# Gated mix of two attention branches: features stored with their sign innermost, key weights transposed while loading, and a new order of steps

## The chip, the core and the metric

The kernel runs on one core of a Trainium2 chip. Its engines work side by side, each through its own queue in order: PE (matmul; a weight load stands before each matmul and may run beside the one ahead), DVE (vector), ACT (activation), POOL (GpSimd), and SP, which issues most of the DMAs. The metric is the device time of one execution in microseconds (us), as a median over runs. The span of a profile is the time from the first instruction of the program to the last.

## What is computed

One input x of 2048 rows by 640 is sent through two attention branches of 32 heads of 20 columns each; a gate for each row mixes the results.

```python
x = A_x
g = _sigmoid((x * gate_w).sum(-1, keepdims=True))
a = _A_ref(x, A_wqkv, A_w_phi, A_wo)        # linear branch
b = _B_ref(x, B_wq, B_wk, B_wv, B_wo, B_beta)   # memory branch
return g * a + (1 - g) * b

# linear branch, for each head
pk = einsum('bhsd,hdf->bhsf', k, w_phi)          # pq likewise
phi_k = concatenate([softmax(pk), softmax(-pk)])  # over the 20 features
kv = einsum('bhsf,bhsd->bhfd', phi_k, v)
z = einsum('bhsf->bhf', phi_k)
o = (phi_q @ kv) / (phi_q @ z + 1e-6)

# memory branch, for each of 4 segments of 512 rows
p = softmax(q @ k.T * scale + causal mask within the segment)
o = sig(beta) * (phi(q) @ M) / (phi(q) @ z) + (1 - sig(beta)) * (p @ v)
M, z = M + phi(k).T @ v, z + sum(phi(k))
```

## The kernel before

The rows of x are cut into 16 chunks of 128; the memory branch works in four segments of four chunks. x is held transposed (`xT`: five blocks of 128 columns by 2048 rows), loaded by transposing DMAs.

All work after the first loads is written as steps. The list `ORDER` (L773) is a hand-fixed sequence of words: the first letter names a function (table `STEPS`, L762), the digit its step, and what follows a PSUM slot or `a` for an eviction on ACT instead of DVE. The n-th occurrence of a word works on the n-th item. Instructions are kept in program order (`Kept`, L98), so the list sets the order on every engine's queue. All instructions are issued through that helper, so the profile shows L104 for nearly all of them, and groups are told apart by the names of their tiles.

Steps of the linear branch (A), by their words:

- T (`transposed`): the key weights `WkN`, loaded plainly, are transposed on PE in 25 blocks and evicted into `WkT`. F and W (`fold`): the key and query weights are multiplied with `w_phi` (`Wphi`, in windows of up to eight heads for each 128 rows), giving `WkA` and `WqA`. The query weights come transposed by DMA (D, `load_q`).
- A (`key`, L244): for each chunk, step 0 projects x with `WkA` (ten matmuls of 320 columns into `k_ps`), steps 1 and 2 take the exponential with scale 1 and -1 on ACT into `Ek`, step 3 sums over a head's 20 features on DVE, step 4 takes the reciprocal, step 5 multiplies into `phk`. B (`value`) projects the values into `vA`, with the row gate as column 321.
- S (`sums`): z, by 160 matmuls of 4 columns with blocks of `phk` as weights (`zb_ps`). s (`blocks`): adds them up on DVE. X (`products`): kv, for each of five blocks of 128 features and each sign 16 matmuls with `phk` as weights (`kv_ps`), masked to the own head's columns by `hm`.
- f (`features`): the query features, kept transposed in `ET`; d (`weights`): denominators; n (`numerators`): for each chunk and half of the heads three matmuls for each sign (`num_ps`).

Steps of the memory branch (B): k, K, v, q project keys, values and queries (`proj`, `q_ps`); P (`scores`) computes causal score blocks `st_ps`, their exponentials on ACT (`PT`, 128 x 1024) and the mask on POOL; V (`attended`) sums with the values (`nd_ps`); Y and M hold the memory term. l, o write the output; t, b, p, a, e, h are the last rows. G, O and J compute gates; I masks.

In `phk` and `Ek` the two signs lie in separate halves. Within a half, the heads are stored in pairs, feature by feature, the two heads of a pair innermost (`"p s (b f i)"`, f = 20, i = 2). The evictions of the folds bring the weights' columns into that order, and the mask `hm` is made from pair masks (`blk`) and a parity (`par`), the latter from the identity matrix that also serves the transposes. A block of 128 stored columns touches eight heads, so the windows of X and n (`WIN`, L163) are eight heads or 160 columns wide (80 where the heads' halves part).

The first loads go out in this order on SP's queue: xT for 128 rows, xT for 384 rows, then L118 to L125: `WkN`, `Wc` (w_phi), `stq` (Wq of the memory branch, which POOL copies in another column order into `WqB`, L159), `WvB`, `WvA`, gate, beta. `WkB` goes out on ACT's queue. L (`load_x`) loads the other three quarters of xT.

Of the kernel before, what the change touches and what calls it, by code (L numbers as in the profile page):

```python
# [8 lines left out]
ALU = mybir.AluOpType  # L9
# [6 lines left out]
def kernel(  # L16
# [64 lines left out]
    phk = apool.tile([P, NCH, 2, D], BF16, name="phk")  # L81
# [3 lines left out]
    late = phk.rearrange("p c s n -> p (c s n)")[:, 16 * D:32 * D]  # L85
    WkN = late[:, 0:KC * D].rearrange("p (c n) -> p c n", c=KC)
# [31 lines left out]
    for out_, in_ in ((WkN, rows5(A_wqkv[:, D:2 * D])),  # L118
                      (Wc, rows5(A_w_phi.rearrange("h f g -> (h f) g"))),
                      (stq, rows5(B_wq)),  # L120
                      (WvB, rows5(B_wv)),
                      (WvA[:, :, 0:D], rows5(A_wqkv[:, 2 * D:3 * D])),
                      (WvA[:, :, D:D + 1], gate_w.rearrange("(c p o) -> p c o", p=P, o=1)),
                      (beta_b, B_beta.partition_broadcast(P))):
        syn.dma_start(out=out_, in_=in_)  # L125

    NW = 8
# [4 lines left out]
    for n in range(WARM):  # L132
        ten.matmul(wu, lhsT=wz[:, 0:P], rhs=wz, start=True, stop=True)
    gps.memset(kpads[:, :, :, DH:32], 0.0)
    ident_f = apool.tile([P, P], F32, name="ident_f")
    gps.memset(ident_f, 0.0)
    gps.affine_select(out=ident_f, in_=ident_f, pattern=[[-1, P]], compare_op=ALU.not_equal,
                      fill=1.0, base=0, channel_multiplier=1)
    gps.memset(kp2[:, :, :, DH:32], 0.0)
    ident = apool.tile([P, P], BF16, name="ident")  # L140
    vec.memset(qTp[0], 0.0)
    vec.tensor_copy(out=ident, in_=ident_f)
# [14 lines left out]
    blk = apool.tile([P, KC, NW // 2], F32, name="blk")  # L157
    band(blk, 8, 2 * DH, NW // 2)
    for c in range(KC):  # L159
        gps.tensor_copy(out=WqB[:, c, :].rearrange("p (r g) -> p r g", g=G),  # L160
                        in_=stq[:, c, :].rearrange("p (g r) -> p r g", g=G))

    WIN = []  # L163
    for c in range(KC):
        lo, hi = 6 * c, 6 * c + NW
        if lo < 16 < hi:
            WIN += [(c, lo, 16), (c, 16, hi)]
        else:
            WIN.append((c, lo, hi))
    FIRST = {w: all((w[1] // 16) != (v[1] // 16) for v in WIN[:n]) for n, w in enumerate(WIN)}  # L170
    LAST = {w: all((w[1] // 16) != (v[1] // 16) for v in WIN[n + 1:]) for n, w in enumerate(WIN)}
# [36 lines left out]
    for k, eps in enumerate((9.98377799987793e-07, 1.622538547962904e-09, -3.410605131648481e-13)):  # L208
        den = Msb.rearrange("p g i e -> p (g i) e")[:, :, DH].rearrange("p (g i) -> p g i", i=4)
        gps.affine_select(out=den, in_=den, pattern=[[0, G], [-32, 4]], compare_op=ALU.not_equal,  # L210
                          fill=eps, base=-(DH + k), channel_multiplier=1)

    gl = const.tile([P, NCH], F32, name="gl")
    par = const.tile([P, 2], F32, name="par")
# [29 lines left out]
    def key(n, step, at, ev):  # L244
# [5 lines left out]
        elif step < 3:  # L250
            if step == 1:
                t.E = a1w.tile([P, 2, D], BF16, name="Ek")
            sca.activation(out=t.E[:, step - 1, :].rearrange("p (a n) -> p a n", a=2),
                           in_=t.ps[:, :, 0:320], func=ACT.Exp, scale=1.0 if step == 1 else -1.0)
        elif step == 3:
            t.Ev = t.E.rearrange("p s (b f i) -> p (s b) f i", f=DH, i=2)
            t.sum = a1w.tile([P, H, 2], F32, name="ksum")
            vec.tensor_reduce(out=t.sum, in_=t.Ev.rearrange("p b f i -> p b i f"),
# [5 lines left out]
        else:  # L264
            vec.tensor_tensor(
                out=phk[:, n].rearrange("p s (b f i) -> p (s b) f i", f=DH, i=2),
# [12 lines left out]

    def transposed(n, step, at, ev):  # L280
        t = item("T", n)
        if step == 0:
            t.ps = bank([P, KC, P], "tp_ps", at, BF16)
            for c in range(KC):
                ten.transpose(out=t.ps[:, c, :], in_=WkN[:, n, c * P:(c + 1) * P], identity=ident)
        else:
            ev(out=WkT[:, :, n * P:(n + 1) * P], in_=t.ps)

    def fold(kind, dst, WT):
        def run(n, step, at, ev):  # L290
# [9 lines left out]
            else:  # L300
                b = step - 1
                ev(out=dst[:, n, b * 320:(b + 1) * 320].rearrange("p (b f i) -> p b i f", f=DH, i=2),
                   in_=t.ps[:, b, 0:320].rearrange("p (b i f) -> p b i f", f=DH, i=2))
        return run

    def masks(n, step, at, ev):
        if step == 0:
            vec.tensor_tensor(
                out=Wphi, in0=Wc[:, :, None, :].to_broadcast([P, KC, NW, DH]),
                in1=hn_f[:, :, :, None].to_broadcast([P, KC, NW, DH]), op=ALU.mult)  # L310
            return
        vec.tensor_reduce(
            out=par, in_=ident_f.rearrange("p (a i) -> p i a", i=2), axis=AX.X, op=ALU.add)
        vec.tensor_tensor(
            out=hm.rearrange("p c (b i) -> p (c b) i", i=2),
            in0=blk.rearrange("p c b -> p (c b)")[:, :, None].to_broadcast([P, KC * NW // 2, 2]),
            in1=par[:, None, :].to_broadcast([P, KC * NW // 2, 2]), op=ALU.mult)
        vec.tensor_copy(out=ind, in_=bd01)
        for sg in range(2):
            vec.tensor_copy(out=HZ[:, :, sg, 0, :], in_=hm)  # L320

    def beta_gate(n, step, at, ev):
        if step == 0:
            sca.activation(out=sig_b, in_=beta_b, func=ACT.Exp, scale=-1.0)
            return
        vec.tensor_scalar(out=sig_b, in0=sig_b, scalar1=1.0, scalar2=None, op0=ALU.add)
        vec.reciprocal(out=sig_b, in_=sig_b)
        vec.tensor_scalar(out=omgh_b, in0=sig_b, scalar1=-1.0, scalar2=1.0,
                          op0=ALU.mult, op1=ALU.add)
        vec.tensor_copy(out=CM[:, :, :, DH:DH + 1],  # L330
                        in_=bd01[:, None, :, None].to_broadcast([P, G, 4, 1]))
        vec.tensor_tensor(
            out=CM[:, :, :, 0:DH],
            in0=sig_b.rearrange("p (g i) -> p g i", i=4)[:, :, :, None].to_broadcast([P, G, 4, DH]),
            in1=bd01[:, None, :, None].to_broadcast([P, G, 4, DH]), op=ALU.mult)

    def token_gate(s, step, at, ev):
        n = slice(4 * s, 4 * s + 4)
        if step == 0:
            sca.activation(out=rgS[:, n], in_=gl[:, n], func=ACT.Exp, scale=-1.0)  # L340
            return
        vec.tensor_scalar(out=rgS[:, n], in0=rgS[:, n], scalar1=1.0, scalar2=None, op0=ALU.add)
        vec.reciprocal(out=omgS[:, n], in_=rgS[:, n])
        vec.tensor_scalar(out=omgS[:, n], in0=omgS[:, n], scalar1=-1.0, scalar2=1.0,
                          op0=ALU.mult, op1=ALU.add)
# [6 lines left out]
    def sums(n, step, at, ev):  # L352
        sgn, half = divmod(n, 2)
        t = item("S", sgn)
        if step == 0:
            if half == 0:
                t.ps = bank([P, KC, 4 * NCH], "zb_ps", at)
            for sc in range(half * NCH // 2, (half + 1) * NCH // 2):
                for c in range(KC):
                    ten.matmul(t.ps[:, c, 4 * sc:4 * sc + 4], lhsT=phk[:, sc, sgn, c * P:(c + 1) * P],  # L360
# [18 lines left out]
    def products(n, step, at, ev):  # L379
        t = item("X", n)  # L380
        c, sgn = divmod(n, 2)
        if step == 0:
            t.ps = bank([P, NW, DH], "kv_ps", at)
            for sc in range(NCH):
                ten.matmul(t.ps, lhsT=phk[:, sc, sgn, c * P:(c + 1) * P],
                           rhs=vA[:, sc, 6 * c * DH:(6 * c + NW) * DH],
                           start=(sc == 0), stop=(sc == NCH - 1))
        else:
            vec.tensor_tensor(out=KV[:, c, sgn], in0=t.ps,
                              in1=hm[:, c, :, None].to_broadcast([P, NW, DH]), op=ALU.mult)  # L390
# [141 lines left out]
    def numerators(n, step, at, ev):  # L532
        s, j, b = n // 8, n % 8 // 2, n % 2
        t = item("n", n)
        if step < 2:
            nm = bank([P, 320], "num_ps", at)
            for w in WIN:
                c, lo, hi = w
                if lo // 16 == b:
                    ten.matmul(nm[:, (lo - 16 * b) * DH:(hi - 16 * b) * DH],  # L540
                               lhsT=item("E", s).t[:, step, c, j * P:(j + 1) * P],
                               rhs=KV[:, c, step, lo - 6 * c:hi - 6 * c, :],
                               start=FIRST[w], stop=LAST[w], skip_group_check=True)
# [208 lines left out]
    def tail_out(j, step, at, ev):  # L752
# [9 lines left out]
    STEPS = dict(A=key, B=value, T=transposed, F=fold("F", WkA, WkT), W=fold("W", WqA, WqT), I=masks,  # L762
# [11 lines left out]
        "k00 k01 k1 k02 k1 K0 K1 k03 k1 k00 K2 k1 k01 k1 k1 T02 I0 T03 k00 T1a T1 T01 k1 F00 F01 "  # L774
        "T1 F1a T02 L0 F1 T03 F2a F2 T1a F00 T1 k00 F1a F2a F01 k1 F00 F1 v01 F1a F2 F2a v02 v1 "
        "k2 K0 K1 A01 v1a K2 L0 v03 A1 A00 v1 A2 A3 A01 A1 A2 D0 A4 q00 A1 A3 A2 k01 q1a A5 A00 "
        "A3 K0 A01 A1 A4 k1 q02 A2 K1 A4 A5 k03 q1a K2 A00 A3 A1 A2 k2 B00 A5 B11 k1 A1 q2 A01 A3 "
        "B2a k2 B3a A2 B02 A4 q2 B4 A4 B13 A3 B2a v00 K0 k2 B01 B3a A5 v1a B12 B2a K1 A00 B4 A5 "
        "A1 B3a A4 A2 K2 v00 A1 B4 A5 W01 q03 A2 A3 v1a W1a B01 W2a A3 B12 q1a B2a A00 q2 B3a A4 "
        "B4 A4 G0 q00 A5 A1 G1 A2 A01 A5 q1a q2 A3 B03 A1 B11 A2 B2 B02 A4 B3a B4 B10 A3 B2a L0 "  # L780
        "W00 W01 B3a B03 B4 W1 W1a W2a W2 B11 A4 B2a W01 B3 A00 B4 W1 W2 A01 A1 A2 q02 A3 W00 v00 "
        "q1a I1 W1a B03 q2 W2a B11 v1a A4 B2a B02 A5 B3a B10 B4 A5 A1 A00 G0 B2 A2 A5 B3a v03 B4 "
        "A1 G1 q01 A3 A2 v1a P01 B02 A3 q1a P1 B10 B03 A4 P2 P3 B2 B11 A4 K0 P4 B3 P01 B2a v02 B4 "
        "A5 B3a P1 B00 K1 B4 A5 B13 P2 P3 v1 A01 B2 B3a P4 B4 G0 G1 J0 A00 A1 J1 A2 B01 A1 B12 A2 "
        "A3 A01 B2a B3a k00 O0 A1 Z0 B4 A3 B03 A2 B11 A4 B2a P00 k1 S02 q2 B3a A3 P1 B03 P2 A4 P3 "
# [90 lines left out]
```

## Time and profile before

| what | value |
|---|---|
| median of 3 runs | 300.85 us (300.8 to 300.87) |
| profiled execution, time | 301.71 us |
| profiled execution, span | 300.0 us |
| granted TensorE clock, mean | 1.00 |
| DMA: bytes, mean rate | 24.51 MB, 82 GB/s |
| chain that ended last, by engine | PE 86%, DMA 6%, ACT 2%, issue 2%, DVE 1%, SP's queue 1% |
| proj / o_ps / nd_ps / st_ps, share of that chain | 14% / 11% / 10% / 9% |
| exponentials of the scores on ACT (160) | 155.5 us busy |
| reduce over features on DVE (16) | 23.4 us busy |

Busy time is the share of the span in which an engine had an instruction in it; engines overlap, so these do not add up to the span. The chain is followed back from the last instruction to whatever released each piece of work; its shares do add up to the span. Weight loads (PEld) overlap the matmuls (PE).

### The profile page before, as it was taken

What the parts mean: (1) busy time and instruction counts of PE and PEld (TensorE: products, weight loads), DVE (VectorE), ACT (ScalarE), POOL (GpSimd) and SP (SyncE); (2) the same over time, 40 slices, a digit from 0 to 9 for tenths busy, and PEclk for the clock granted to TensorE, in tenths of its full rate; (3) what the DMA queues carried; (4) which work ended last, traced back from release to release, by engine and by line L of the source; (5) the groups of instructions that cost most, each with busy time, mean ns of one, the idle gap of its engine ahead of it and who ended that gap; (6) DMA issues with size and microseconds to landing.
All of it is one profiled execution on the core that took longest, in us unless ns stands there. A gap on an engine that the chain in (4) does not pass through costs nothing.

```text
span 300.0 us, 9652 instructions
## 1 busy us (share of the span) xinstructions
PE 291.4 (97%) x3913; PEld 197.9 (66%) x3913; DVE 233.4 (78%) x604; ACT 240.6 (80%) x337; POOL 180.0 (60%) x362
## 2 busy tenths in 40 slices
PE   7899999999999999999899999999999999999994
PEld 3676767667788656667466776566667657667672
DVE  3889997989738548988778989849999846889713
ACT  1467776788878699899899879999989998999721
POOL 5193000034664554699676699766899965899830
PEclk9999999999999999999999999999999999999999
DMA  8999807000000094337205303913534123303803
GB/s 200 320 226 225 131 17 108 17 2 0 21 4 3 12 264 87 73 68 121 62 12 71 86 8 74 118 31 62 79 64 55 39 68 67 69 24 69 187 13 110
DMA packets 63148, 24.51 MB, mean 82 GB/s; under 512 B 54016, under 2 KB 63104, under 8 KB 63104
## 3 DMA queue, kind: packets, MB, share of 16 engines
q1 hardware_dynamic: 62160, 22.75, 38.4%
q10 hardware_dynamic: 944, 1.15, 1.2%
q8 instruction: 30, 0.49, 0.7%
q14 instruction: 14, 0.11, 0.1%
HBM read 5.77 MB, written 2.62 MB: 28 GB/s over the span
## 4 chain that ended last, share of the span: by engine, by line
PE 86%; DMA 6%; ACT 2%; issue 2%; DVE 1%; SPq 1%; POOLq 0%; POOL 0%; DVEq 0%
PE proj L104 14%; PE o_ps L104 11%; PE nd_ps L104 10%; PE st_ps L104 9%; PE v_ps L104 7%; PE k_ps L104 7%; PE q_ps L104 6%; PE pf_ps L104 6%; PE num_ps L104 4%; PE kv_ps L104 4%; PE mem_ps L104 3%; DMA kTs<-kpads 2%; DMA xT<-in_A_x_dram 2%; ACT PT L104 2%; PE zb_ps L104 1%
## 5 line engine op out<-in xcount | busy, mean ns | idle before, releaser
L104 ACT ACTIVATE PT<-st_ps 128x1024 bf16<-128x1024 f32 x160 | 155.5, 1029 | 19.8 <-PE st_ps L104 18.6
L104 POOL TENSOR_SCALAR_AFFINE_SELECT PT<-PT 128x256 bf16<-128x256 bf16 (+1 forms) x224 | 99.3, 461 | 76.9 <-ACT PT L104 75.3
L104 PEld LDWEIGHTS <-xT 128*128 128x128 bf16 x640 | 60.1, 98 | 28.5 <-issue 3.4
L104 PEld LDWEIGHTS <-PT 128*128 128x128 bf16 x1280 | 36.2, 96 | 3.5 <-issue 1.0
L104 PE MATMUL nd_ps<-vB,PT 128*128 128x32 bf16 x1280 | 37.3, 177 | 0.1
L104 PE MATMUL st_ps<-qTp,kTs 32*128 32x384 bf16 (+3 forms) x512 | 34.6, 300 | 0.5 <-ACT PT L104 0.2
L104 DVE TENSOR_TENSOR t<-num_ps,dd 128x320 f32<-128x320 f32 x64 | 28.7, 484 | 2.6 <-PE num_ps L104 1.1
L104 PEld LDWEIGHTS <-oT 128*128 128x128 bf16 x240 | 22.1, 98 | 11.2 <-issue 3.0
L104 POOL TENSOR_TENSOR oA<-t,t 128x320 bf16<-128x320 f32 x32 | 28.2, 883 | 1.0 <-DVE t L104 0.9
L104 ACT ACTIVATE Ek<-k_ps 128x640 bf16<-128x640 f32 x32 | 21.2, 704 | 8.8 <-PE k_ps L104 5.7
L104 PE MATMUL proj<-WvB,xT 128*128 128x320 bf16 x160 | 26.5, 299 | 0.9 <-DVE qd L104 0.9
L104 PE MATMUL proj<-WkB,xT 128*128 128x320 bf16 x160 | 26.2, 299 | 0.9 <-DMA xT<-in_A_x_dram 0.8
L104 POOL TENSOR_TENSOR oB<-td,tm 128x320 bf16<-128x320 f32 (+2 forms) x25 | 21.4, 859 | 6.9 <-DVE td L104 6.9
L104 DVE TENSOR_REDUCE ksum<-Ek 128x64 f32<-128x1280 bf16 x16 | 23.4, 1475 | 1.8 <-ACT Ek L104 1.8
L104 PEld LDWEIGHTS <-kTs 32*128 32x128 bf16 (+1 forms) x552 | 13.7, 92 | 16.9 <-issue 12.0
L104 PE MATMUL q_ps<-xT,WqB 128*128 128x512 bf16 x100 | 24.6, 380 | 0.2 <-DVE mtmp L104 0.2
L104 PE MATMUL pf_ps<-xT,WqA 128*128 128x512 bf16 x100 | 24.6, 380 | 0.0
L104 PE MATMUL v_ps<-WvA,xT 128*128 128x320 bf16 (+1 forms) x160 | 24.0, 300 | 0.0
L104 PE MATMUL k_ps<-qTp,xT 128*128 128x320 bf16 x160 | 23.7, 299 | 0.0
L104 ACT ACTIVATE ET<-pf_ps 128x512 bf16<-128x512 f32 x40 | 21.8, 632 | 0.3 <-PE pf_ps L104 0.2
L104 PEld LDWEIGHTS <-phk 128*128 128x128 bf16 x375 | 18.4, 97 | 3.2 <-issue 1.7
L104 DVE CAST kpads<-proj 128x320 bf16<-128x320 f32 x28 | 13.5, 482 | 9.1 <-PE proj L104 5.6
(111 smaller groups left out, 458.5 us busy)
## 6 DMA issues: line engine op xcount, KB each, us to landing
out_dram<-osb SPq DMA_DIRECT2D x12, 160.0 KB
qTp<-qd SPq DMA_DIRECT2D x8, 128.0 KB
WkB<-in_B_wk_dram ACTq DMA_DIRECT2D x1, 800.0 KB
phk<-in_A_wqkv_dram SPq DMA_DIRECT2D x1, 800.0 KB
vA<-in_B_wq_dram SPq DMA_DIRECT2D x1, 800.0 KB
WvB<-in_B_wv_dram SPq DMA_DIRECT2D x1, 800.0 KB
WvA<-in_A_wqkv_dram SPq DMA_DIRECT2D x1, 800.0 KB
WoA<-in_A_wo_dram SPq DMA_DIRECT2D x1, 800.0 KB
```

Of the source, the lines that this page charges most:

```text
L104: return lambda *a, **k: kept(f(*a, **k))
```

## The change

- `phk` and `Ek` are stored as head, feature, sign: the two signs are neighbours, and a head's 20 features are 40 consecutive elements. ACT writes each sign's exponentials at every second element; S and X read their weights at every second element. DVE's three steps work on arrays of the same shape, with the sign in the place that the head of a pair had.
- The folds' evictions no longer permute columns. The masks come straight from the head mask `hn_f`; `ident`, `par` and `blk` are gone.
- X and n use the windows of the fold (`ROWS`): seven heads, 140 columns, for four blocks of 128 features; eight heads, 160 columns, for the middle one in X, and 4 + 4 heads for it in n.
- The key weights are loaded by a transposing DMA straight into `WkT`; the steps T are gone.
- The loads behind xT go out in the order `Wc`, `WvB`, `WkT`, `WvA`, gate, beta, `stq`; POOL's five copies into `WqB` stand behind its fills for the first segment.
- The steps G, I and J are cut into one instruction each, and `ORDER` is a new sequence. Seven more evictions of the linear branch's values stand on DVE instead of ACT.

```diff
-    phk = apool.tile([P, NCH, 2, D], BF16, name="phk")
+    phk = apool.tile([P, NCH, D, 2], BF16, name="phk")
...
-    for out_, in_ in ((WkN, rows5(A_wqkv[:, D:2 * D])),
-                      (Wc, rows5(A_w_phi.rearrange("h f g -> (h f) g"))),
-                      (stq, rows5(B_wq)),
-                      (WvB, rows5(B_wv)),
-                      (WvA[:, :, 0:D], rows5(A_wqkv[:, 2 * D:3 * D])),
+    syn.dma_start(out=Wc, in_=rows5(A_w_phi.rearrange("h f g -> (h f) g")))
+    syn.dma_start(out=WvB, in_=rows5(B_wv))
+    syn.dma_start_transpose(out=WkT, in_=A_wqkv[:, D:2 * D])
+    for out_, in_ in ((WvA[:, :, 0:D], rows5(A_wqkv[:, 2 * D:3 * D])),
                       (WvA[:, :, D:D + 1], gate_w.rearrange("(c p o) -> p c o", p=P, o=1)),
-                      (beta_b, B_beta.partition_broadcast(P))):
+                      (beta_b, B_beta.partition_broadcast(P)),
+                      (stq, rows5(B_wq))):
         syn.dma_start(out=out_, in_=in_)
...
-                t.E = a1w.tile([P, 2, D], BF16, name="Ek")
-            sca.activation(out=t.E[:, step - 1, :].rearrange("p (a n) -> p a n", a=2),
+                t.E = a1w.tile([P, D, 2], BF16, name="Ek")
+            sca.activation(out=t.E[:, :, step - 1].rearrange("p (a n) -> p a n", a=2),
                            in_=t.ps[:, :, 0:320], func=ACT.Exp, scale=1.0 if step == 1 else -1.0)
...
-                out=phk[:, n].rearrange("p s (b f i) -> p (s b) f i", f=DH, i=2),
+                out=phk[:, n].rearrange("p (h f) s -> p h f s", f=DH),
                 in0=t.Ev, in1=t.rec[:, :, None, :].to_broadcast([P, H, DH, 2]), op=ALU.mult)
...
-                ten.transpose(out=t.ps[:, c, :], in_=WkN[:, n, c * P:(c + 1) * P], identity=ident)
...
-                ev(out=dst[:, n, b * 320:(b + 1) * 320].rearrange("p (b f i) -> p b i f", f=DH, i=2),
-                   in_=t.ps[:, b, 0:320].rearrange("p (b i f) -> p b i f", f=DH, i=2))
+                ev(out=dst[:, n, b * 320:(b + 1) * 320], in_=t.ps[:, b, 0:320])
...
-                    ten.matmul(t.ps[:, c, 4 * sc:4 * sc + 4], lhsT=phk[:, sc, sgn, c * P:(c + 1) * P],
+                    ten.matmul(t.ps[:, c, 4 * sc:4 * sc + 4], lhsT=phk[:, sc, c * P:(c + 1) * P, sgn],
...
+        lo, hi = min(w[1] for w in ROWS if w[0] == c), max(w[2] for w in ROWS if w[0] == c)
...
-                ten.matmul(t.ps, lhsT=phk[:, sc, sgn, c * P:(c + 1) * P],
-                           rhs=vA[:, sc, 6 * c * DH:(6 * c + NW) * DH],
+                ten.matmul(t.ps, lhsT=phk[:, sc, c * P:(c + 1) * P, sgn],
+                           rhs=vA[:, sc, lo * DH:hi * DH],
...
-            for w in WIN:
-                c, lo, hi = w
-                if lo // 16 == b:
-                    ten.matmul(nm[:, (lo - 16 * b) * DH:(hi - 16 * b) * DH],
+            for m, (c, lo, hi) in enumerate(ROWS[3 * b:3 * b + 3]):
+                ten.matmul(nm[:, (lo - 16 * b) * DH:(hi - 16 * b) * DH],
...
-        "k00 k01 k1 k02 k1 K0 K1 k03 k1 k00 K2 k1 k01 k1 k1 T02 I0 T03 k00 T1a T1 T01 k1 F00 F01 "
-        "T1 F1a T02 L0 F1 T03 F2a F2 T1a F00 T1 k00 F1a F2a F01 k1 F00 F1 v01 F1a F2 F2a v02 v1 "
+        "k00 k01 k1 k1 k02 J4 K0 k03 K1 k1 k00 K2 k1 k01 k1 K0 K1 k02 k1 K2 v03 K0 K1 k1 v00 I0 "
+        "v1a v01 v1a K2 v02 L0 v1 v03 v1 F00 v1 k00 F1a F2a F01 k1 v01 F1 K0 F2 F00 k2 v02 K1 v1a "
...
```

## The prediction

> **What bounds the kernel now.** I read the busy times by engine first, then the same by stage (columns after the stretch: its length, then busy time and count of PE, PE weight loads, DVE, ACT, POOL; granted clock; DMA share; GB/s), then the chain that ended last, then the groups by shape.
>
> ```profile
> PE 291.4 (97%) x3913; PEld 197.9 (66%) x3913; DVE 233.4 (78%) x604; ACT 240.6 (80%) x337; POOL 180.0 (60%) x362
> ...
> 6.20:16.00 9.80, 8.95 (x93) 6.67 (x94) 7.47 (x17) 3.81 (x7) 2.23 (x2) 1.00 1.07 316
> ...
> 32.00:78.00 46.00, 46.00 (x390) 31.30 (x388) 42.02 (x88) 36.43 (x72) 8.42 (x10) 1.00 0.25 40
> ...
> 116.00:250.00 134.00, 132.85 (x1928) 87.32 (x1921) 111.20 (x307) 123.71 (x162) 103.76 (x213) 1.00 0.36 62
> 250.00:300.00 50.00, 45.56 (x670) 31.41 (x667) 33.51 (x88) 33.61 (x40) 32.78 (x63) 1.00 0.35 81
> ```
>
> PE has work queued nearly always, at full granted clock in each stretch. From 32 to 78 us (keys and values of the linear branch) DVE has 4.0 us left and ACT 9.6; from 116 to 250 ACT has 10.3 left. A busy PE is not PE at its peak, so I took the chain's pieces, whose lengths are real advance:
>
> ```profile
> 24.17 2.72 PE k_ps L104 x20
> ...
> 80.73 0.98 PE zb_ps L104 x40
> ...
> 96.94 1.11 PE kv_ps L104 x16
> ```
>
> Twenty matmuls of 320 columns take 2.72 us, 136 ns each; sixteen of 160 take 1.11, 69.4 each; forty of 4 columns take 0.98, 24.5 each. So a column costs (136 - 69.4)/160 = 0.416 ns, and PE's time follows columns except where they are very few. Adding, from the trace's start times, the advance of each step of the order list at the shortest usual value of its kind gives 279.7 us; steps exceed it by 15.3 us in all: 1.5 from 6 to 16 us, 1.9 from 16 to 116, 6.9 from 116 to 250, 5.0 after 250. Columns removed are thus time removed, and 15 us depend on the order.
>
> **What goes off PE.** *Products:* four of five chunks move 140 columns instead of 160. The middle one still covers eight heads, so 128 of 160 matmuls shrink: 128 x 20 x 0.416 ns = 1.07 us. *Numerators:* the 128 wide ones shrink alike: another 1.07. *Transposes of the key weights:* 25 matmuls go.
>
> ```profile
> 11.34 0.56 PEld L104 LDWEIGHTS <-phk 128*128 128x128 bf16 x10 [0.89 <-DMA phk<-in_A_wqkv_dram]
> 11.34 0.73 PE L104 MATMUL tp_ps<-ident,phk 128*128 128x128 bf16 x10 [0.56 <-DVE phk L104]
> ...
> 11.91 0.30 PE L104 MATMUL proj<-WkB,xT 128*128 128x320 bf16 x1
> ```
>
> Ten start at 11.34 and the next projection at 11.91: 57 ns each, 1.4 us for 25. Sum off PE: 1.07 + 1.07 + 1.4 = **3.5 us**. The five evictions and the identity's building go too, off the path.
>
> **The start.** The bracketed 0.89 above is a wait for the plain load of the key weights; it becomes a wait for a transposing load behind WvB on SP's queue.
>
> ```profile
> 13.78 7.25 POOL L104 COPY WqB<-vA 128x640 bf16<-128x640 bf16 x5 [8.73 <-DMA vA<-in_B_wq_dram]
> ...
> 24.58 3.62 SPq L104 DMA_TRANSPOSE vA<-in_A_wqkv_dram  x1
> ```
>
> Successive 800 KB loads land at 11.3 and 13.7, so one takes 2.4 us; the transposing load of the same size, issued at 24.58, completes at 30.1, 3.7 us after the transfer ahead of it (completion events of the trace). WvB takes the place of the first plain load and lands near 11.3, WkT near 15.0 by estimate. All of PE stands behind F0 on its queue; with eight projections of Wk and five of Wv moved ahead (0.68 us each; kept as cover), it comes to F0 at 14.4 plus today's 0.3 us wait for xT: a wait of 0.3 us. If all the waits of the 6 to 16 stretch went, 1.5 would be gained; if WkT landed as late behind its predecessor as the first xT load behind its issue (5.7 us), 2.0 more would be lost. I take a gain of 0.7. The Wq load goes behind WvA, gate and beta: WvA 17.4, the small ones 17.7, Wq 20.1, the five POOL copies (7.25 us) done at 27.4; the first query projection stands at 28.2 in added-up time, so 0.8 us plus the delay met by then covers it. The x loads, key transposes and WqT load behind it on SP come about 1.3 us later; WqT near 28.4, used at 32.4. Uncovered, each us late is one us of PE.
>
> **Strided access.** Products and sums now load weights at every second element: 160 + 160 loads; no load of before is strided. Bounds: nothing, as a 160-column matmul already hides its load (69.4 ns of which 66.6 are columns); or no hiding of the recorded 97 ns of a load. In the sums 4 columns hide nothing: up to 160 x (97 - 24.5) = 11.6 us; in the products 128 x (97 - 61) + 32 x (97 - 69) = 5.5. I take 0: the nearest row, 24.5 ns for 128 weight columns, is far below one column at a time (53 ns at 0.416), so several are read at once in parts, which a step of two need not break. [...]
>
> ACT now writes the exponentials at every second element.
>
> ```profile
> L104 ACT ACTIVATE Ek<-k_ps 128x640 bf16<-128x640 f32 x32 | 21.2, 704 | 8.8 <-PE k_ps L104 5.7 <-DVE phk L104 1.1 <-ACT qd L104 1.0
> ...
> L104 ACT CAST vA<-v_ps 128x320 bf16<-128x320 f32 x25 | 10.5, 434 | 2.2 <-PE v_ps L104 2.0
> ...
> L104 ACT CAST qTp<-fold_ps 128x320 bf16<-128x320 f32 x6 | 2.7, 527 | 1.4 <-PE fold_ps L104 1.4
> ```
>
> The fold's eviction, written in steps of two, takes 527 ns against 434 packed: 93 for 320 elements, 186 for 640; 32 x 186 = 6.0 us of ACT at most, nothing at least. Seven evictions of the linear branch's values go from ACT to DVE by the order list and give back 7 x 0.43 = 3.0, two transpose copies 1.4, twelve packed fold copies 1.1. Net near zero, inside the 9.6 us that ACT has there: nothing on the path. DVE reads and writes the same shape in the same memory order: nothing. DVE takes those seven (0.40 each back to back, 2.8 us) and loses three transpose copies (1.2).
>
> **The order.** With the back-to-back durations of the rows (reduce 1.39, reciprocal 0.46, multiply 0.73, eviction 0.40), the new order gives DVE 40.8 us of work beside 40.3 of PE between 30 and 70 us of added-up PE time, where before it was 35.2 beside 39.3. Bounds: 0, or with the 5% that DVE's recorded busy time exceeds such sums now, 2.5. I take a loss of 0.5. The first score matmul moves from 58.7 to 49.9 of added-up time, so ACT's 160 big exponentials (155.5 us) spread over more time; the last one moves from 269.5 to 265.8, with 11.4 us behind it as before. Bounds: a gain of 3 (a fifth of 15.3), a loss of 3. I take a gain of 0.5. Finer steps for gates and masks add no work.
>
> **Sum.** Span 300.0 - 3.5 - 0.7 + 0.5 - 0.5 = 295.8. The profiled execution took 301.71, 1.71 around its span, and stands 0.86 above the median of 300.85; so the median becomes 300.85 - 4.2 = **296.7 us**.
>
> **Rivals.**
>
> *A, slower: strided weight loads lose their speed.* Place: sums and products, 72 to 101 us. For it: the sums run at 24.5 ns with nothing to hide a longer load. Against: the parts argument above. It cancels the gain once the two groups lose 4.2 us, which is a load of some 51 ns in the sums with the products still covered. At 53 ns: 160 x 28.5 = 4.6 us, 301.3; at 97, 17.1 more, 313.8. Between them, nearer the first: 304.
>
> *B, the new order eats the saving.* For it: DVE at 101% of PE beside it, a 5.4 us stretch between the last query eviction and the first score that must hold eviction, two issues of 0.7 us and a landing of 2 to 4 us, and after 236 us the score steps already advance at 2.49 us against 2.24 of added-up PE time, so columns saved there are worth less. Against: the same number of steps, ACT 4 us lighter after the first scores. Price: 2.5 for DVE and 1 for the queries instead of 0.5 and -0.5: 300.2.
>
> *C, the order gives more:* the 3 us bound: 294.2 after 296.7 + 0.5 - 3. For it: ACT's load per PE time between first score and the last 20 falls from 0.90 to 0.89 (sums of the same durations), and 6.9 us of stalls lie there. Against: so small a change of load.
>
> *D, the change misses part of what it says:* were PE's spacing not by columns in numerators, whose groups are only three matmuls long, 1.07 would stay: 297.8; it lies within the forecast's range.
>
> **Chances.** Forecast (with D) 0.52, B 0.18, C 0.10, A 0.20. No change means within 0.2% or 0.6 us: 300.25 to 301.45. Forecast and C are faster: 0.62; of B 0.06 faster, 0.07 no change, 0.05 slower; A slower. Faster 0.68, same 0.07, slower 0.25. The forecast's own range is 294.5 to 299.0. The range for all, 293.6 to 302.8, holds the forecast, B, most of C and the low part of A (0.08); what is left out is the long tail of A.
>
> **What would show it.** Right: products at about 61 ns, sums still at 24.5, numerator steps 18 ns shorter each, no transposes; PE waits for the key weights under 1 us near 15 us; first scores near 52 us; ACT's Ek between 704 and 890 ns. Wrong: sums above 45 ns or products above 70 (A); PE waiting for DVE evictions between 30 and 75 us, or for qTp before the first score (B); a query projection waiting on POOL's copies near 29 us.

## The result, and the profile after

Over seven runs each, interleaved on one chip, the changed kernel has a median of **302.72 us** (301.93 to 303.91), the kernel before 300.87 (300.73 to 301.52): ratio 1.0065, 95% interval 1.0043 to 1.0087, some 1.9 us slower. The profiled execution took 302.43 us with a span of 300.7.

First the busy times and the chain that ended last, from the page of the changed kernel:

```profile
PE 289.7 (96%) x3867; PEld 195.2 (65%) x3888; DVE 235.1 (78%) x607; ACT 238.8 (79%) x327; POOL 177.8 (59%) x357
...
PE 72%; DVE 8%; DMA 6%; SPq 5%; ACT 4%; issue 2%; POOL 1%; POOLq 0%; DVEq 0%; ACTq 0%
```

PE is busy 1.7 us less, as columns went, but its share of the chain fell from 86% to 72%: DVE (1% before, now 8%), SP's queue (1%, now 5%) and ACT (2%, now 4%) hold what PE held. The stages (columns as before: length, then busy time and count of PE, PE weight loads, DVE, ACT, POOL; granted clock; DMA share; GB/s) show where:

```profile
6.20:16.00 9.80, 9.53 (x70) 6.50 (x70) 7.41 (x18) 3.18 (x6) 0.68 (x3) 1.00 1.05 245
16.00:32.00 16.00, 14.84 (x120) 10.42 (x120) 13.08 (x27) 10.84 (x21) 7.48 (x5) 1.00 0.97 211
32.00:78.00 46.00, 44.75 (x416) 30.48 (x416) 42.72 (x81) 37.16 (x63) 11.50 (x20) 1.00 0.34 56
116.00:250.00 134.00, 132.14 (x1931) 87.34 (x1944) 110.58 (x306) 122.08 (x163) 99.85 (x204) 1.00 0.34 66
```

The first stretch is better filled than before (9.53 of 9.80; it was 8.95). But from 16 to 78 us 2.4 us are now idle, where PE had been busy throughout; from 32 to 78 the prediction shows that, from 16 to 32 this line of the kernel before:

```profile
16.00:32.00 16.00, 16.00 (x117) 10.99 (x115) 15.54 (x22) 11.06 (x20) 8.89 (x11) 1.00 1.10 211
```

Adding up the step list as the prediction did: shortest advances 276.7 us (279.7 before), excess over them 19.0 (15.3). So 3.0 us came off PE's work and 3.7 us went into waits: between 16 and 78 us the excess is 4.1 instead of 0.5. These lines of the timeline show them (start, length, engine, work; in brackets the idle time ahead and what ended it):

```profile
23.80 7.48 POOL L103 COPY WqB<-vA 128x640 bf16<-128x640 bf16 x5 [16.78 <-DMA vA<-in_B_wq_dram]
...
31.34 1.47 PE L103 MATMUL q_ps<-xT,WqB 128*128 128x512 bf16 x6 [1.11 <-POOL WqB L103]
...
42.31 0.58 ACT L103 CAST qd<-q_ps 128x512 bf16<-128x512 f32 x1 [1.60 <-DMA qTp<-qd]
...
43.60 0.47 PE L103 MATMUL fold_ps<-phk,vA 128*128 128x140 bf16 x6 [1.03 <-ACT WqA L103]
```

POOL copied Wq from 23.8 to 31.3 us, and the first query projection stood 1.11 us for it. Next, ACT stood 1.60 us before it could evict a query tile, since the DMA that reads the buffer's last tile was still out; the fold behind stood 1.03 us for ACT. A third place comes later, at the first denominators (two answers: PE, then ACT):

```profile
122.61 0.28 PE L103 MATMUL dn_ps<-HZ,ET 128*128 128x16 bf16 x5 [0.53 <-ACT ET L103]
```

```profile
120.92 1.15 ACT L103 ACTIVATE eq<-qTp 128x512 bf16<-128x512 bf16 x2 [2.01 <-DMA qTp<-qd]
```

ACT stood 2.01 us at a word of Y that needs a query DMA; the `ET` evictions are behind it, and PE needs those. About 1 us of PE goes.

The strided loads of weights cost nothing, the strided writes something. From the chain (sums), and from the groups by shape (exponentials):

```profile
88.11 0.98 PE zb_ps L103 x40
```

```profile
L103 ACT ACTIVATE Ek<-k_ps 128x640 bf16<-128x640 f32 x32 | 25.8, 896 | 7.6 <-issue 2.0 <-PE k_ps L103 2.0 <-DVE gl L103 1.5
```

Forty sums still take 0.98 us, 24.5 ns each; by the starts in the trace, products and numerators of 140 columns follow each other at 61 ns and those of 160 at 69. Only ACT's exponentials got longer, from 704 to 896 ns.

### The profile page after: what moved, and what is told of

It reads as the page before. It is cut to its first block, busy times and chain, and to the rows that moved or that the text cites. A ratio compares the mean times of both kernels' runs of the same rounds, so it can differ in the third digit from the quotient of the medians.

```text
span 300.7 us, 9571 instructions
## 1 busy us (share of the span) xinstructions
PE 289.7 (96%) x3867; PEld 195.2 (65%) x3888; DVE 235.1 (78%) x607; ACT 238.8 (79%) x327; POOL 177.8 (59%) x357
## 4 chain that ended last, share of the span: by engine, by line
PE 72%; DVE 8%; DMA 6%; SPq 5%; ACT 4%; issue 2%; POOL 1%; POOLq 0%; DVEq 0%; ACTq 0%
PE proj L103 12%; PE nd_ps L103 10%; PE o_ps L103 10%; PE st_ps L103 9%; PE pf_ps L103 5%; PE v_ps L103 5%; SPq L103 5%; PE q_ps L103 5%; PE num_ps L103 4%; PE kv_ps L103 4%; DMA qTp<-qd 3%; PE k_ps L103 3%; PE mem_ps L103 2%; ACT PT L103 2%; DVE ksum L103 2%
## 5 line engine op out<-in xcount | busy, mean ns | idle before, releaser
L103 ACT ACTIVATE PT<-st_ps 128x1024 bf16<-128x1024 f32 x160 | 155.8, 1033 | 22.2 <-PE st_ps L103 20.1
L103 POOL TENSOR_SCALAR_AFFINE_SELECT PT<-PT 128x256 bf16<-128x256 bf16 (+1 forms) x224 | 98.2, 456 | 71.6 <-ACT PT L103 70.0
L103 PE MATMUL st_ps<-qTp,kTs 32*128 32x384 bf16 (+3 forms) x512 | 35.7, 300 | 0.9 <-ACT PT L103 0.6
L103 ACT ACTIVATE Ek<-k_ps 128x640 bf16<-128x640 f32 x32 | 25.8, 896 | 7.6 <-issue 2.0
L103 PEld LDWEIGHTS <-kTs 32*128 32x128 bf16 (+1 forms) x552 | 14.3, 92 | 18.2 <-issue 13.7
L103 PE MATMUL k_ps<-qTp,xT 128*128 128x320 bf16 x160 | 23.7, 299 | 0.0
L103 PE MATMUL o_ps<-WoA,oT 128*128 128x320 bf16 x120 | 20.3, 300 | 0.0
```

The source lines that it names most:

```text
L103: return lambda *a, **k: kept(f(*a, **k))
```

## The experiments

All edits start from the kernel before or the changed kernel, all ratios are to the kernel before on the same chip (its medians there: 301.1 to 301.4 us). "Excess" is what PE's steps take beyond the shortest advance of their kind, from the profile.

### Which part loses: storage, load or order

**a_layout**: kernel before with the new storage, masks and windows alone; loads, T and the order are the old ones.

```diff
-    phk = apool.tile([P, NCH, 2, D], BF16, name="phk")
+    phk = apool.tile([P, NCH, D, 2], BF16, name="phk")
```

> The kernel before with the new storage of features alone: strided writes and weight loads, 140-column products and numerators, packed fold evictions; the transposes on PE, the loads and the order of steps stay. Theory O (the new order and loads lose the saving, the storage is a gain): PE loses 2.1 us of columns (128 + 128 matmuls by 8.3 ns) and the 192 ns that each of 32 exponentials grows (704 to 896 in the profile after) are covered by ACT's idle time: 298.7, between 298.0 and 299.6. Theory E (the longer exponentials break the key stage): 6.1 us more of ACT cost what the columns save or more: 300.5 to 304.

Measured 300.21 us (299.77 to 301.58, 12 runs), ratio 0.9971 [0.9959, 0.9984]. The storage alone is a gain, though 0.9 us, not the 2.1 that its columns are worth.

```profile
L104 ACT ACTIVATE Ek<-k_ps 128x640 bf16<-128x640 f32 x32 | 26.1, 891 | 6.6 <-PE k_ps L104 4.5 <-DVE phk L104 0.9 <-ACT qd L104 0.7
```

`Ek` takes 891 ns here too, so in the old order strided writing costs ACT 187 ns for 640 elements (192 in the changed kernel); what ends ACT's idle time is still mostly PE. The cost is nearly covered, not quite: in the profile, which is of the slowest of the 12 runs, PE idles 0.38 us from 16 to 78 us (15.85 of 16 and 45.77 of 46 busy), before not at all.

**b_dmat**: kernel before with the key weights transposed by the load, in the place of the plain load, and without T.

```diff
-    for out_, in_ in ((WkN, rows5(A_wqkv[:, D:2 * D])),
+    syn.dma_start_transpose(out=WkT, in_=A_wqkv[:, D:2 * D])
```

> The kernel before with the key weights turned by the loading DMA, at the place in the queue where the plain load stood; the transpose steps are dropped, everything else stays. If the transposing load costs only its own 1.3 us more than a plain one: 25 matmuls of 57 ns and the stalls between them go, up to 2 us gained: 299.0 to 300.0. If the load holds up SP's queue (5.6 us of issue in the profile after) so that the loads behind it come 3 us later: values and queries wait at 16 to 26 us, 301 to 304.

Measured 303.69 us (303.57 to 305.18, 5 runs), ratio 1.0083 [1.0069, 1.0098]: 2.5 us slower, though 25 transposes are gone. From its timeline, and from its stages:

```profile
6.18 3.87 SPq L103 DMA_TRANSPOSE phk<-in_A_wqkv_dram  x1
...
10.09 0.59 SPq L103 DMA_DIRECT2D Wc<-in_A_w_phi_dram  x1
...
13.54 0.99 DVE L103 TENSOR_TENSOR phk<-Wc,hn_f 128x800 bf16<-128x800 bf16 x1 [1.38 <-DMA Wc<-in_A_w_phi_dram]
...
14.59 0.79 PE L103 MATMUL fold_ps<-phk 128*128 128x140 bf16 x12 [2.21 <-DVE phk L103]
```

```profile
15.51:18.93 3.42, 2.89 (x22) 2.29 (x22) 1.47 (x4) 1.39 (x4) 2.47 (x2) 0.50 1.06 376
```

The first fold stands 2.21 us, but not for the key weights: by the completion events of the trace their load landed at 12.14 us, 3.4 us after the block of x ahead of it, as the plain load did in the kernel before (11.29, also 3.4). It stands for `Wphi`, which DVE makes from `Wc`; the load of `Wc` stands behind the transposing one, whose issue held SP for 3.87 us, and went out at 10.09 instead of 6.53. The loads behind it landed 2.0 to 2.9 us later than before. Behind the wait PE's granted clock is 0.50 for 3.4 us (last section), which costs up to 1.7 more. The changed kernel loads `Wc` ahead of the transposing load; no run tried that with the old order.

**c_oldlayout**: changed kernel with the old storage (160-column windows, permuting evictions).

```diff
-    phk = apool.tile([P, NCH, D, 2], BF16, name="phk")
+    phk = apool.tile([P, NCH, 2, D], BF16, name="phk")
```

> The changed kernel with the storage of features of before: packed writes and weight loads, 160-column products and numerators, permuting fold evictions; loads and order of steps are the new ones. Theory O: 2.1 us of columns come back and the order's stalls stay: 304 to 305.5. Theory E: ACT is relieved of 6 us in the key stage and the time falls below the changed kernel's 302.7 in spite of the columns: 299 to 302.

Measured 305.52 us (303.5 to 306.69, 6 runs), ratio 1.0134 [1.0108, 1.016]. Loads and order alone cost 1.34%, 4.0 us; in this order the storage is worth 0.69%, 2.1 us, though some of that is a fall of the clock, which four of these six runs had and two of the seven of the changed kernel (last section). So the loss sits in loads and order, and the longer `Ek` is not its cause.

### Which wait of the new order: late Wq, buffers, Y

**d_wq** and **f_wqmid**: Wq loaded earlier; d ahead of `WvA`, f ahead of beta only, with five words of beta's gate (J0 to J3 and J5) moved later.

```diff
+    for out_, in_ in ((stq, rows5(B_wq)),
+                      (WvA[:, :, 0:D], rows5(A_wqkv[:, 2 * D:3 * D])),
-                      (stq, rows5(B_wq))):
```

> The changed kernel with the query weights of the memory branch (Wq) loaded ahead of WvA instead of last. In the profile after, Wq lands at 23.7 us, POOL's copies end near 31.3 and the first query projection waits 1.3 us, with ACT then waiting for query buffers (2.7 us). If the late Wq is the main cause: Wq lands near 18, the waits go, 299.5 to 301.3. If it is not: the values wait for WvA instead, or the time is merely moved: 302 to 303.5.

> The changed kernel with Wq loaded ahead of beta instead of behind it (WvA and gate keep their places), and the five instructions that make the beta gates moved some twenty steps later. Wq should land near 21 us instead of 23.7, POOL's copies end near 28.7, and the 1.3 us wait of the first query projection go, with the queries 1 to 2 us earlier. If the late Wq costs what its wait shows: 301.0 to 301.9. If the stretch to 78 us is bound by DVE, the time only moves to another wait: 302.4 to 303.

d: 304.5 us (303.26 to 306.03, 6 runs), ratio 1.0104 [1.0078, 1.0129]: the waits at 29 and 41 us are gone, but `WvA` and the gate are late (PE waits 1.3 us for them near 21 us), and the clock fell in five of the six runs. f: 303.39 us (303.19 to 303.79, 6), 1.0074 [1.0056, 1.0091]: Wq landed at 23.3, hardly earlier than the 23.7 of the changed kernel; the first query waits no more, yet PE stands 1.49 us before 40.7 us for DVE's `kpads`, ahead of which the moved gate instructions now run (0.82 us for `CM` alone). Both move the wait and gain nothing.

**e_bq**: three query buffers of their own for the first segment (`qa`; it had used the two of `qd`). **g_d01**: the first words of Y moved behind those of f and d. **h_all**: e, f and g.

```diff
-            t.qd = bq.tile([P, L], BF16, name="qd")
+            t.qd = (a1w.tile([P, L], BF16, name="qa", bufs=3) if s == 0 else
+                    bq.tile([P, L], BF16, name="qd"))
...
-        "... V1 Y0 Y1 P4 V2 k03 V3 Y0 Y2 f1 Y1 P01 k1 f2 v00 Y2 K0 K1 d01 ..."
+        "... V1 P4 V2 k03 V3 f1 P01 k1 f2 v00 Y0 Y1 Y2 K0 K1 d01 v1 Y0 P1 Y1 Y2 ..."
```

> The changed kernel with three query buffers of their own for the first segment (from the linear branch's pool), five buffers instead of two. In the profile after, ACT waits 2.7 us in three places for a query buffer whose DMA has not landed, with the fold's evictions behind it, and PE loses 1.2 us at 41 us. If that queueing is on the path: 0.8 to 1.6 us less, 301.1 to 301.9. If DVE sets the pace there anyway: 302.4 to 303.

> The changed kernel with the first two groups' query features of the memory branch (words Y) moved behind the last exponentials of the linear branch's features (words f), so that ACT does not wait for a query DMA with those exponentials behind it; PE loses 1.4 us at 121 us there in the profile after. If the stall is worth itself: 301.3 to 302.0. If it also sets off the fall of the granted clock to 0.5 for 3.4 us that runs with a mean clock of 0.992 to 0.994 show, up to 1.7 us more in those runs: median 300.3 to 301.3, and no run of it below 0.997. If it only moves: 302.4 to 303.

> The three edits together: five query buffers in the first segment, Wq ahead of beta, query features behind the feature exponentials. If the new order loses by these waits, their sum goes: 298.5 to 300.3, below the kernel before. If the order is bound by DVE up to 78 us and by ACT behind it: 301.5 to 303.

e: 302.22 us (301.54 to 303.26, 10 runs), 1.0038 [1.0023, 1.0053]. g: 302.71 us (302.08 to 303.66, 6), 1.0052 [1.0032, 1.0071], with the denominators in one piece and no wait:

```profile
121.76 1.15 PE L103 MATMUL dn_ps<-HZ,ET 128*128 128x16 bf16 x40
```

h: 302.08 us (301.19 to 302.8, 12), 1.0026 [1.0013, 1.004], with f's wait for `kpads` in it. Each wait named is real, none is the whole.

**i_evict, j_bqd01, k_bqd01evict**: i moves the first seven DVE evictions of values back to ACT (`B2` to `B2a`); j is e and g; k is j and i.

> The changed kernel with the seven value evictions that it moved from ACT to DVE back on ACT; nothing else. Theory (DVE overfull between 30 and 78 us): DVE's busy time in 32 to 78 us falls by about 2.5 us from 42.7, ACT's rises by 3, and the time falls by 0.5 to 1.5 us from 302.7 to 301.2 to 302.2; most of the stall near 29 and 41 us stays, since Wq and the two query buffers cause it. Rival (ACT, with its longer Ek and the waits for query buffers, is as full as DVE there): no gain or a loss, 302.7 to 303.5.

> The changed kernel with own query buffers for the first segment and the first memory-query words behind the feature words (the two mended waits together, without the later gate words). Both alone gave 302.2 and 302.7. If the waits add up, 301.7 to 302.2 and no stretch at half clock near 121 us; if what was waited for only hid DVE's fullness, 302.2 to 302.7, with DVE 96% busy or more between 32 and 78 us.

> The same two mends with the seven value evictions back on ACT. Theory (DVE is the bound of 32 to 78 us once the waits are mended): 0.8 to 1.8 us below the run without that edit, near 300.7, with DVE about 92% busy there. Rival (ACT bound): equal to it or above, 302 to 303.

i: 303.81 us (302.87 to 305.88, 6 runs), 1.0083 [1.0057, 1.0109]. j: 301.32 us (300.64 to 301.84, 11), 0.9995 [0.9985, 1.0004]. k: 301.32 us (300.8 to 302.09, 11), 1.0003 [0.9993, 1.0013]. Two mended waits return 0.70%, 2.1 us, where e and g singly add up to 0.40%; better than j's expectation. Part of the surplus is the clock, which fell in half of e's runs and in none of j's. Lightening DVE returns nothing, with them or without. That DVE's fullness sets the time finds no support here.

### The same queue of waits, followed to its end

**l_qlater**: j, with the first two query projections some key steps later on the list.

```diff
-        "... B3a A5 q02 B4 A3 A1 A2 q03 k2 q1a A5 A01 L0 I1 I2 A4 q1a ..."
+        "... B3a A5 B4 A3 A1 A2 k2 A5 A01 q02 L0 I1 I2 A4 q03 q1a A3 k00 q1a ..."
```

> The run with the two mends (own query buffers, memory-query words behind the feature words) and, besides, the first two query projections each some steps later on the list, so that one or two key projections (1.36 us each) stand ahead of them while POOL copies the query weights. Theory (the 1.1 us wait of the first query projection for POOL's copies is a true loss of PE): 0.8 to 1.3 us off 301.3, so 300.0 to 300.5, below the kernel before. Rival (DVE is full there, PE only waits elsewhere, as in the run with the later gate words): 301.0 to 301.8, the wait gone at 30 us and new excess between 32 and 78 us.

Measured 301.18 us (300.88 to 302.03, 11 runs), ratio 1.0001 [0.9992, 1.001]; no gain. PE's wait for POOL is gone, but at 46 us:

```profile
46.03 0.58 ACT L103 CAST qa<-q_ps 128x512 bf16<-128x512 f32 x1 [1.28 <-DMA qTp<-qa]
```

With three buffers the fourth tile waits for the first one's DMA. **m_five** uses five (three own, two common), **n_fiveevict** also i's edit:

```diff
-            t.qd = (a1w.tile([P, L], BF16, name="qa", bufs=3) if s == 0 else
+            t.qd = (a1w.tile([P, L], BF16, name="qa", bufs=3) if s == 0 and c < 3 else
```

> The last run with five buffers for the five query tiles of the first segment (three own ones and the two common ones) instead of three. In the last run ACT waited 1.28 us at 46.0 us for a query tile's DMA and PE 1.04 us behind it. Theory (the first segment's queries, crowded behind the late query weights, are what the new order lost there): both waits near 30 and 46 us are gone, excess between 16 and 50 us under 0.4 us, and 0.7 to 1.1 us off 301.2, so 300.1 to 300.5. Rival (DVE is full in that stretch and PE must wait for it somewhere): 300.9 to 301.4, with a new wait for DVE between 32 and 78 us.

> The same with the seven value evictions back on ACT. If DVE is the bound with all waits mended: 0.5 us or more below the run without that edit. If not: equal to it within 0.3 us, or above.

m: 302.42 us (301.28 to 303.53, 12 runs), 1.0035 [1.002, 1.0051]. n: 304.14 us (302.41 to 304.76, 6), 1.0073 [1.0046, 1.01]. m fits neither of its expectations; n is above m, in part by the clock, which fell in four of its six runs and in four of m's 12. The timeline of m (ACT and PE):

```profile
50.27 0.59 ACT L103 CAST qd<-q_ps 128x512 bf16<-128x512 f32 x1 [1.83 <-DMA qTp<-qd]
...
53.48 0.39 PE L103 MATMUL st_ps<-qTp,kTs 32*128 32x512 bf16 x2 [1.39 <-ACT Ek L103]
```

Tiles four and five now hold the common buffers, so the first tile of the second segment waits 1.83 us; `Ek` and the value evictions stand behind it on ACT, and PE behind them. DVE has no part in it. **o_six** gives that tile an own buffer too; **p_sixevict** is o and i:

```diff
-            t.qd = (a1w.tile([P, L], BF16, name="qa", bufs=3) if s == 0 and c < 3 else
+            t.qd = (a1w.tile([P, L], BF16, name="qa", bufs=3) if n < 3 or n == 5 else
```

> The last but one with one more change of buffers: the sixth query tile (first of the second segment) goes into the own buffers too. With five buffers ACT waited 1.83 us at 50.3 us to evict that tile, since the buffer's DMA was still out, and PE 1.78 us behind ACT. Theory (a queue of waits for query tiles, which moves on to the next tile as each is mended): no ACT wait for a query DMA is left before the first score, excess from 16 to 78 us at most 1.0 us, and 300.0 to 300.5. Rival (DVE is full): 300.9 to 301.5, excess from 16 to 78 us above 1.5 us, PE released by DVE.

> The same with the seven value evictions back on ACT: DVE lighter by 2.8 us, ACT heavier by 3.0, no query wait to hold ACT. If DVE were the bound: 0.5 us or more below the run without that edit. If ACT's queue is as tight: equal to it within 0.3 us, or above.

o: **299.74 us** (299.08 to 301.1, 12 runs), ratio 0.9958 [0.9945, 0.997]. p: 300.13 us (299.8 to 300.32, 6), 0.9966 [0.9955, 0.9978]. The theory of a queue of waits is borne out: the excess from 16 to 78 us is 1.04 us in o (4.06 in the changed kernel), and no ACT wait for a query's DMA is left there. Stages and chain of o:

```profile
16.00:32.00 16.00, 16.00 (x131) 11.43 (x129) 13.10 (x29) 10.80 (x21) 7.48 (x5) 1.00 0.96 203
32.00:78.00 46.00, 45.99 (x435) 31.08 (x433) 45.19 (x86) 39.23 (x65) 14.62 (x25) 1.00 0.35 59
```

```profile
PE 83%; DVE 5%; DMA 3%; ACT 2%; SPq 2%; issue 2%; POOL 1%; POOLq 0%; DVEq 0%; ACTq 0%
```

PE idles no more in these stages, though DVE is busy 45.19 us of 46: a full DVE did not bind. p, with 2.4 us less of DVE's time from 16 to 78 us, wins nothing. So o beats both kernels, with the whole change in it and four edits to the waits.

## Why the prediction was wrong

**What bounds the kernel, and columns.** Right. The shortest advances sum to 276.7 us in the changed kernel and 276.1 in o, 3.0 and 3.6 below the kernel before, against a forecast of 3.5. The transposes cost 57 ns each and are gone; products and sums measured 61 and 24.5 ns. That strided loads of weights cost nothing, which the prediction held against its rival A, is shown by a_layout and the changed kernel alike (25 ns median between sums in both); rival A falls. The reading "in parts" from which it was argued stays an inference from the 24.5 ns.

**The start.** Roughly right, with luck in it: the excess before 16 us fell from 1.53 to 0.61, 0.9 for a forecast of 0.7, though the first matmul of the list came 0.39 us later. `WkT` landed at 14.81 us, estimated 15.0, but two errors met there: `WvB` landed at 11.92 instead of 11.3, and `WkT` 2.9 us behind it instead of 3.7. The 3.7 was read between the first completion events of the two transfers (26.46 and 30.12); between the last ones (27.22 and 30.22) it is 3.0. Whether the projections moved ahead are what makes the late weights bearable is not shown: b_dmat lacks them, but its wait was for `Wc`.

**Strided writes on ACT.** Bounded at 704 to 890 ns, measured 896, just above; nearly off the path, as said (0.38 us of idle PE in a_layout).

**The failed step** is the part that followed the loads and the order: "Wq 20.1, the five POOL copies (7.25 us) done at 27.4", and with it "I take a loss of 0.5" and "a gain of 0.5" for the order. Wq landed at 23.7, and the copies ended at 31.3. The working put the transfers end to end. By the completion events `WkT` came at 14.8 (worked 15.0), `WvA` at 18.2 (17.4), beta at 20.2 (17.7), Wq at 23.7 (20.1): 0.8 us went at `WvA`, 1.7 more at the two small loads, 1.1 more at Wq itself. These are stages of the changed kernel; the last column is what the DMA moved, in GB/s:

```profile
16.00:17.00 1.00, 1.00 (x13) 0.81 (x12) 0.50 (x3) 0.64 (x2) 0.00 (x0) 1.00 1.05 370
17.00:18.00 1.00, 1.00 (x13) 0.81 (x12) 1.00 (x4) 0.85 (x2) 0.00 (x0) 1.00 0.46 59
18.00:19.00 1.00, 1.00 (x13) 0.81 (x12) 0.90 (x3) 0.86 (x3) 0.00 (x0) 1.00 0.06 4
```

The DMA was nearly still from 17 to 19 us although Wq had been issued at 14.56. Why it stood is open.

The working also left out that the transposing load holds SP's queue while it is issued, here for 5.55 us; it had the loads of x and the key transposes behind it "about 1.3 us later". The rows, before and after:

```profile
5.89 0.59 SPq L104 DMA_DIRECT2D phk<-in_A_wqkv_dram  x1
...
19.32 2.24 SPq L104 DMA_TRANSPOSE kTs<-kpads  x1
```

```profile
7.21 5.55 SPq L103 DMA_TRANSPOSE phk<-in_A_wqkv_dram  x1
...
14.56 0.43 SPq L103 DMA_DIRECT2D vA<-in_B_wq_dram  x1
15.03 8.95 SPq L103 DMA_TRANSPOSE xT<-in_A_x_dram  x1
24.11 1.23 SPq L103 DMA_TRANSPOSE kTs<-kpads  x1
```

The plain issue took 0.59 us, the transposing one 5.55, and the 3.62 us row that the prediction quoted for its landing was itself such an issue. The next block of x went out at 15.03, 1.4 us later than before, but its issue took 8.95 us instead of 5.53, and the first key transpose came 4.8 us later. For Wq the hold can't be the whole cause: Wq was issued over 3 us before `WvA` had landed.

The five queries of the first segment, which the old order spread out between 22 and 52 us and the new one packs between 29 and 40, then met two buffers, and again SP's queue:

```profile
31.76 0.58 ACT L103 CAST qd<-q_ps 128x512 bf16<-128x512 f32 x1
...
33.10 4.57 SPq L103 DMA_TRANSPOSE xT<-in_A_x_dram  x1
...
37.78 1.24 SPq L103 DMA_TRANSPOSE kTs<-phk  x1
...
39.12 0.68 SPq L103 DMA_DIRECT2D qTp<-qd  x1
```

The first tile was evicted by 32.3 us, but its DMA was issued at 39.12, behind a block of x and a key transpose, which the new order puts ahead of it. So most of the ten us for which a buffer was held went by before its DMA began; in the chain of l one such DMA itself took 3.40 us. No run moved the block of x; the runs that end the waits do it by more buffers. This chain (load, POOL copy, projection, eviction, SP's queue, DMA, buffer) holds the two largest waits from 16 to 78 us, 1.29 and 1.20 us of excess. I had priced the queries' share at 1 us within rival B and at nothing in the forecast.

How much of the miss that is: the forecast was 0.986 of the kernel before, the measured ratio 1.0065, 6.1 us apart. With the waits mended (o, 0.9958) 3.2 of them come back.

**Rival B** named the right stretch and the right chain ("eviction, two issues of 0.7 us and a landing"), but charged most to DVE. i, k, n and p take work off DVE and gain nothing; its 101% of PE was harmless, since in this stretch PE stood still for ACT, POOL and, in f and h, for one late DVE eviction. B's 300.2 was also too low. **C** and **D**: the order gave nothing; numerators shrank by columns, so D falls.

What stays open is the other 2.9 us: with nearly all waits up to 78 us mended, o is 1.3 us faster by the medians, not the 4.2 forecast; its profiled execution, its fastest at 299.08 us, has a span of 297.3 us against 300.0. Its shortest advances are as forecast, its excess is 16.2 us against 15.3 before (7.9 between 116 and 250 us, before 6.9), in many small pieces. No run took these apart.

## What to carry to other kernels

The transposing load of the key weights was paid for twice in these runs: in its transfer (it landed 3.4 us after the transfer ahead of it in b_dmat and 2.9 in the changed kernel, the plain load 3.4 in the kernel before), and in the time for which its issue held SP's queue (3.87 and 5.55 us, the plain issue 0.59); what stood behind it on that queue went out only then (`Wc` in b_dmat 3.6 us later). Before crowding steps that go through a DMA, count the buffers between eviction and DMA against the whole time to the landing, the wait for the queue included (some ten us for a query buffer of the changed kernel). A wait there stopped everything else on the evicting engine (1.83 us of ACT in m, with `Ek` and the value evictions behind it), and mending one buffer showed the next (the wait at 46.0 us in l, at 50.3 in m). And a neighbour that is 98% busy (DVE in o, 45.19 of 46 us) is not yet a bound: take work off it and see.

## What the runs showed of the hardware

**The granted clock fell behind stretches with little matmul work.** In four of the 18 profiles PE's granted clock is 0.50 for exactly 3.413 us in mid-run; all stretches at full clock between two changes are whole multiples of 3.413 us (119.466 is 35, 174.080 is 51). One of the four, around 123 us in d_wq:

```profile
116.00:123.24 7.24, 5.87 (x103) 3.79 (x103) 3.90 (x13) 4.72 (x9) 0.82 (x2) 1.00 0.49 112
123.24:126.65 3.41, 3.41 (x25) 1.55 (x21) 3.41 (x7) 2.66 (x4) 1.54 (x4) 0.50 0.02 5
126.65:134.00 7.35, 7.30 (x102) 4.59 (x100) 6.25 (x18) 6.90 (x11) 3.48 (x9) 1.00 0.24 57
```

I cut all 18 profiles into windows of 3.413 us from the moment at which full clock was first granted, some 1500 windows without the last ones, in which the work runs out, and summed for each the columns moved times 0.416 ns (the prediction's figure for a column) times the share of the 128 rows in use. The four windows ahead of the drops are the four lowest: 0.21 (b_dmat), 0.27 (d_wq), 0.27 (i_evict), 0.30 (n_fiveevict) of the window; the lowest without a drop is 0.40. By busy time alone they don't stand out (0.31 to 0.62, with others at 0.53 to 0.60 that were not followed by a drop). The four windows held 1.3 to 2.4 us without matmuls, in three of the four beside matmuls of few columns or few rows. That a share between 0.30 and 0.40 parts the windows rests on four events; no run set it on purpose.

One kernel has runs with and without a drop: e_bq took 301.5 to 302.1 us in runs with a mean clock of 0.997 to 0.999, 302.4 to 303.3 at 0.993 to 0.994; what decides between them is not shown. A mean clock of 0.994 or less is found in two of seven runs of the changed kernel (the other five have a median of 302.43, so some 0.3 us of its 1.9 is the clock), three of five of b, four of six of c, five of six of d, five of ten of e, one of six of f, two of six of i, four of 12 of m and four of six of n; in no run of a, g, h, j, k, l, o and p. It is part of the loss of those kernels.

**Issue time of transposing loads.** 800 KB took SP 3.87 us in b_dmat and 5.55 in the changed kernel, where the next block of x then took 8.95 (5.53 before); the plain issue of the same weights took 0.59. Some plain issues were long too: 2.30 us for `WvA` before, 2.74 for beta in b_dmat. In b_dmat the load landed as soon after the transfer ahead of it as the plain one (3.4 us each); in the changed kernel the DMA moved 290 GB/s from 12 to 14 us, where the transposing load ran, and 370 from 16 to 17, where a plain one did.
